# Moving the decay of v, the first state decays and most low weight halves of layer 1 from VectorE and ScalarE to GpSimd

## The chip, the cores and the metric

The kernel runs on one core of a Trainium2 chip. The metric is device time in microseconds (us) of one execution; a smaller number is better. Profiles are taken of one execution, and their times count from its first instruction. TensorE is called PE, VectorE DVE, ScalarE ACT, GpSimd POOL, and SyncE, which issues most transfers, SP.

## The reference, cut to what matters

```python
# q, k, v: (8, 8, 576, 64) f32;  w_in: (512, 2048), w_out: (2048, 512), both float64
scores = q @ k.T / 8
gamma = 1 - 2 ** (-5 - arange(8))                      # one per head
ret = scores * where(i >= j, gamma ** (i - j), 0)      # retention, no softmax
x = (ret @ v), heads side by side                      # 4608 tokens x 512
h = x @ moe_w_in;   x = (h - tanh(h)) @ moe_w_out      # layer 1
h = x @ moe2_w_in;  out = (h * sigmoid(1.702 h)) @ moe2_w_out   # layer 2
```

## The kernel before

**Retention.** A batch's 576 positions are cut into five chunks (four of 128, the last of 64), 40 chunks in all, worked off in order. For each chunk `att_load` issues transfers of kT, qT, v and k. `att_decay` multiplies v in place by one factor for each row and head (`dg`). `att_scores` multiplies q by k on PE into `pj` and masks the scores into `pm` on DVE (L321). `att_values` makes `op` on PE from the old state, `pm` and v (L334), makes the update `up` from k and v (L348), adds it to the state S (L352) and multiplies S by the decay over a chunk (L353); the next chunk's `op` reads that S. The result times `dq` becomes a part of x: kept in `xf` for the first 512 tokens (L362), else written through `xe` (L367) to `xd` in memory. The constant `LEAD` is 4: four chunks are done ahead of layer 1, the others piece by piece between its steps. In `att_decay` the first 8 chunks (2 * LEAD) are one DVE instruction each (L295); the later ones are 8 (in a batch's last chunk 4) ACT instructions (L300).

**Layer 1.** x is split into two f16 halves, `xh` (ACT, L186) and `xl` (DVE, L187); each weight likewise into a high half (`wih`, `woh`) and a low half (`wil`, `wol`), and each product takes three matmuls (L464 into h, L626 into y). Tokens go in nine tiles of 512; a tile has eight steps, and a step needs one pair of blocks of `w_in` (kind "i") and, two steps later, one of `w_out` (kind "o"). The weights arrive as 64-bit words of 1 MB for each of 16 units. `unit_load` issues the transfer into `f` (two buffers). `unit_join` puts the words together into f32 `w` (two buffers) with ACT (L176, for "o" also L180) and DVE (L178 for "i", L181, L182). `unit_split1` then makes the high half on ACT and the low half on DVE, through `two` (L186, L187). This conversion runs inside the first token tile: two units at each step until all 16 are done; two of the units come ahead of the first step. After tanh's on ACT (L477, L478), a step's `wt` is a DVE product (L482), and is split into `gh` (ACT) and `gl` (DVE).

**Order.** A planner puts each engine's instructions in a fixed order ahead of time, by the program's order and by when it expects operands to be ready. On the chip an engine works off its list in that order: an instruction whose operand is late holds up all behind it on its engine. `newest`, `pin` and `after` are tiny copies that make an instruction wait for another one's result, to hold it in its place. GpSimd has 18 instructions in the whole program; two of them (L158, tiny copies) hold back weight loads until a part of `xf` is there.

**Layer 2** starts near 830 us; its weights are converted by other functions, which the change leaves alone.

Of the kernel before, what the change touches and what calls it, by code (L numbers as in the profile page):

```python
# [17 lines left out]
AF = mybir.ActivationFunctionType  # L18
ALU = mybir.AluOpType
# [5 lines left out]
B, H, S, D = 8, 8, 576, 64  # L25
NT, DM, DFF = 4608, 512, 2048
P = 128
# [4 lines left out]
NPAIR = H // 2  # L32
CHUNKS = [(s0, min(P, S - s0)) for s0 in range(0, S, P)]
# [18 lines left out]
SW = 2.0**13  # L52
# [3 lines left out]
LEAD = 4  # L56
# [39 lines left out]
def small_h(ctx: ExitStack, tc: tile.TileContext, w1i, w1o, w2i, w2o, qt, kt, k, v, dq_d,  # L96
            dv_d, mask_d, dg_d, out, flag):
    nc = tc.nc
    V, A, G, PE, SP = nc.vector, nc.scalar, nc.gpsimd, nc.tensor, nc.sync
# [85 lines left out]
    def two(hi, lo, src, scale):  # L185
        A.activation(out=hi, in_=src, func=AF.Copy, scale=scale)  # L186
        V.scalar_tensor_tensor(out=lo, in0=src, scalar=scale, in1=hi, op0=ALU.mult, op1=ALU.subtract)  # L187

    def unit_split1(kind, p):
        o, w = L[1], L[1].raw.pop((kind, p))  # L190
        if kind == "i":
            b, u = divmod(p, 2)
            if not u:
                o.wih[b], o.wil[b] = (wp1.tile([P, KD, 512], F16, tag=f"{nm}{b}", name=f"{nm}1_{b}") for nm in ("wih", "wil"))
            hi, lo = (x[b][:, :, u * 256 : u * 256 + 256] for x in (o.wih, o.wil))
        else:
            b, u = divmod(p, 4)
            if not u:
                o.woh[b], o.wol[b] = (wp1.tile([P, 8, DM], F16, tag=f"{nm}{b}", name=f"{nm}1_{b}") for nm in ("woh", "wol"))
            hi, lo = (x[b][:, 2 * u : 2 * u + 2, :] for x in (o.woh, o.wol))  # L200
        two(hi, lo, w, SW)

    def unit_most1(kind, p):
        o = L[1]
# [61 lines left out]
    def ps_tile(pp, stage, name):  # L266
        p, tag = pp[stage]
        return p.tile([P, NPAIR, P], F32, tag=tag, name=name)

    def ps_two(pp, stage, name):  # L270
        p, tag = pp[stage]
        return p.tile([P, 2, NPAIR, P], F32, tag=tag, name=name)
# [17 lines left out]
    def att_decay(b, n):  # L290
        s0, T = CHUNKS[n]
        a = att[b, n]
        if b * len(CHUNKS) + n < 2 * LEAD:
            x, w = (0, H) if T == P else (H, NPAIR)
            V.tensor_tensor(out=a.v[:, :w], in0=a.v[:, :w], op=ALU.mult,  # L295
                            in1=dg[:, x : x + w].rearrange("p (a b) -> p a b", b=1).to_broadcast([P, w, D]))
            return
        for h in range(H if T == P else NPAIR):
            x = h if T == P else H + h
            A.activation(out=a.v[:, h], in_=a.v[:, h], func=AF.Copy, scale=dg[:, x : x + 1])  # L300

    def att_scores(b, n, pp, pin=None):
        s0, T = CHUNKS[n]
# [20 lines left out]
    def att_values(b, n, pp):  # L324
        s0, T = CHUNKS[n]
        a = att.pop((b, n))
        op = ps_two(pp, "v", "op")
        state = att.get((b, "S"))

        def add(w, x, c0, c1, start, stop):  # L330
            for hp in range(NPAIR):
                q, c = divmod(hp, 2)
                for j in range(2):
                    PE.matmul(op[64 * c : 64 * c + 64, j, q, c0:c1], w(hp, j), x(hp, j), start=start and not q, stop=stop and q == 1)  # L334

        half = lambda j: slice(64 * j, 64 * j + 64)
        if n:
            add(lambda hp, j: state[half(j), hp, :], lambda hp, j: a.qT[half(j), hp, :T], 0, T, True, False)
        if T == P:
            add(lambda hp, j: a.v[half(j), NPAIR * j + hp, :], lambda hp, j: a.p[j][half(j), hp, :64], 0, 64, not n, False)  # L340
            add(lambda hp, j: a.v[:, NPAIR * j + hp, :], lambda hp, j: a.p[j][:, hp, 64:], 64, P, False, True)
        else:
            add(lambda hp, j: a.v[half(j), hp, :], lambda hp, j: a.p[0][half(j), hp, :T], 0, T, not n, True)
        if n + 1 < len(CHUNKS):
            up = ps_tile(pp, "u", "up") if pp is not late else op[:, 0, 2:].rearrange("p a (b d) -> p (a b) d", b=2)
            for hp in range(NPAIR):
                for j in range(2):
                    PE.matmul(up[half(j), hp, :D], a.k[:, NPAIR * j + hp, :], a.v[:, NPAIR * j + hp, :], start=True, stop=True)  # L348
        if n + 1 < len(CHUNKS):
            new = ap.tile([P, NPAIR, D], F32, tag="S", name="S")  # L350
            if n:
                V.tensor_tensor(out=new, in0=up[:, :, :D], in1=state, op=ALU.add)  # L352
            V.tensor_tensor(out=new, in0=new if n else up[:, :, :D], op=ALU.mult,  # L353
                            in1=dg[:, H + NPAIR :].rearrange("p (a b) -> p a b", b=1).to_broadcast([P, NPAIR, D]))
            att[b, "S"] = new
        by_bank = lambda x, at: x.rearrange("p (j q) t -> p j q t", j=2)[:, :, :, at : at + T]
        done, g0 = 0, b * S + s0
        if g0 + T <= TT:

            if not x_first:  # L360
                x_first.append(yp.tile([P, KD, TT], F32, tag="yf", name="xf"))
            V.tensor_tensor(out=by_bank(x_first[0], g0), in0=op[:, :, :2, :T], in1=by_bank(dq, 0), op=ALU.mult)  # L362
            return
        e = ap.tile([P, NPAIR, P], F32, tag="xe", name="xe", bufs=1)
        if n + 1 < len(CHUNKS):
            V.tensor_copy(out=e[:, 0, :1], in_=new[:, 0, :1])
        V.tensor_tensor(out=by_bank(e, 0), in0=op[:, :, :2, :T], in1=by_bank(dq, 0), op=ALU.mult)  # L367
        while done < T:
            ti, off = divmod(g0 + done, TT)
            m = min(T - done, TT - off)  # L370
            SP.dma_start(x_d[ti][:, :, off : off + m], e[:, :, done : done + m])
            done += m
# [293 lines left out]
    dg = ac.tile([P, H + 2 * NPAIR], F32, name="dg")  # L666
# [11 lines left out]
    early = {"s": (ps_y, "y"), "v": (ps_a, "a"), "u": (ps_h, "h")}  # L678
# [3 lines left out]
    units1 = deque([("i", 0), ("i", 1), ("o", 0)])  # L682
# [8 lines left out]
    def next_join(after=None):  # L691
        unit_join(1, *units1[0], wb, after)
        next_load()

    def next_split():
        unit_split1(*units1.popleft())

    warm = cp.tile([P, TT], F16, name="warm")
    V.memset(warm, 0.0)
# [21 lines left out]
    for i in range(-2, LEAD):  # L721
        if i + 2 < LEAD:
            att_decay(*chunks[i + 2])
        if 0 <= i + 1 < LEAD:
            att_scores(*chunks[i + 1], early)
        if i >= 0:
            att_values(*chunks[i], early)
            if i == 0:
                att_load(*beyond[NIP])
                for x in range(2):  # L730
                    next_load(tp, x_first[0][:1, x, :1])
            if i in (1, LEAD - 1):
                fill(att[0, "S"][:1, 0, :1], 5 if i == 1 else 12)
        if i == 2:
            after = [att[0, LEAD - 1].p[-1][:1, 0, :1]]
# [2 lines left out]
        pre.popleft()()  # L738
    for i in range(2):
        next_join(after[i])  # L740
        next_split()
    for i in range(1, LEAD):
        att_load(*beyond[i + NIP])
    bg = deque()
    for i, ch in enumerate(chunks[LEAD:]):
        def begin(ch=ch, nxt=beyond[LEAD + i + NIP - 1] if i else None):
            if nxt:
                att_load(*nxt)
            att_decay(*ch)

        bg.append(begin)
        pp = middle if i < 2 else late
        pin = (lambda: att[0, "S"][:1, 0, :1], lambda: newest[0][:1])[i] if i < 2 else None
        bg.append(lambda ch=ch, pp=pp, pin=pin: att_scores(*ch, pp, pin))
        bg.append(lambda ch=ch, pp=pp: att_values(*ch, pp))
# [6 lines left out]
    for i in range(n1 + LAG):  # L762
        if i < n1:
            t, p = steps[i]
# [3 lines left out]
            for _ in range(2 if len(pre) > KF // 2 - p else 1):  # L768
                if pre:
                    pre.popleft()()  # L770
            work = [f for _ in range(2 if units1 else 0) for f in (next_join, next_split)]
            if bg:
                n = min(6 if t == 0 else 5, len(bg))
# [46 lines left out]
        if i >= LAG:  # L820
            t, p = steps[i - LAG]
# [4 lines left out]
    for n in range(LAG, NTILE * KF // 2):  # L826
        t, p = divmod(n, KF // 2)
# [827 lines left out]
```

## Time and profile before

| | us |
|---|---|
| median of 3 runs | 1558.76 (1558.08 to 1559.37) |
| the profiled execution: its own time | 1558.13 |
| its span, first to last instruction | 1556.4 |
| PE busy in the span | 1531.8 (98%) |
| DVE busy | 1082.1 (70%) |
| ACT busy | 823.1 (53%) |
| POOL busy | 4.9 (0%) |

The profiled execution's own time is 1.7 us over its span, and 0.6 us under the median of the runs. Busy shares are averages over stages with different limits; the time in which PE stands still is 24.6 us in the whole span.

### The profile page before, as it was taken

How to read it: one execution, taken by the hardware profiler on the slowest of the kernel's cores; microseconds unless marked ns; L12 is line 12 of the kernel's file. 1: busy time of each engine (PE TensorE's matmuls, PEld its weight loads, DVE VectorE, ACT ScalarE, POOL GpSimd, SP SyncE). 2: the span in 40 equal slices, each digit the busy share in tenths (PEclk: the TensorE clock that was granted, in tenths of full speed). 3: DMA queues.
4: the chain of work that ended last, by engine and by line, in shares of the span. 5: the costliest groups of instructions: out<-in, count | busy, mean ns of one | idle time of the engine just before them, and what ended most of it. 6: DMA issues, size and time to landing. Idle time of an engine off the chain costs nothing.

```text
span 1556.4 us, 29515 instructions
## 1 busy us (share of the span) xinstructions
PE 1531.8 (98%) x12347; PEld 1024.0 (66%) x12347; DVE 1082.1 (70%) x1720; ACT 823.1 (53%) x1441; POOL 4.9 (0%) x18
## 2 busy tenths in 40 slices
PE   7999999999999999999999999999999999999998
PEld 4444555555554544444444588888888888888887
DVE  6984535554443438888776499797888888887865
ACT  3995545455455446778676455354544454454432
POOL 0000000000000000000000000000000000000000
PEclk9999999999999999999999999999999999999999
DMA  9663324233323124444428243433434433432310
GB/s 356 219 197 123 118 74 155 73 105 109 112 79 106 51 92 138 170 162 156 158 101 310 85 150 116 152 123 123 150 119 127 141 127 119 140 129 99 133 62 30
DMA packets 107983, 205.84 MB, mean 132 GB/s; under 512 B 24640, under 2 KB 47808, under 8 KB 105664
## 3 DMA queue, kind: packets, MB, share of 16 engines
q1 hardware_dynamic: 107552, 203.72, 39.4%
q8 instruction: 99, 1.62, 0.4%
q14 instruction: 44, 0.36, 0.1%
q10 hardware_dynamic: 288, 0.14, 0.0%
HBM read 161.88 MB, written 41.94 MB: 131 GB/s over the span
## 4 chain that ended last, share of the span: by engine, by line
PE 91%; ACT 3%; DVE 1%; DMA 1%; issue 0%; ACTq 0%; SPq 0%; DVEq 0%
PE y L626 22%; PE h L464 22%; PE pr L520 21%; PE yp L555 20%; PE op L334 2%; PE pj L316 2%; PE yk L555 1%; PE op L348 1%; DMA f<-in_moe_w_out 1%; ACT w L176 1%; ACT v L300 0%; ACT u L481 0%; ACT u L477 0%; ACT wih L186 0%; ACT w L180 0%
## 5 line engine op out<-in xcount | busy, mean ns | idle before, releaser
L520 PEld LDWEIGHTS <-ws 128*128 128x128 f16 x3024 | 295.9, 98 | 36.5 <-issue 1.7
L464 PE MATMUL h<-xh,wih 128*128 128x512 f16 x576 | 218.2, 379 | 2.2 <-ACT wih L186 1.9
L464 PE MATMUL h<-xl,wih 128*128 128x512 f16 x576 | 218.2, 379 | 0.8 <-DVE xl L187 0.8
L626 PE MATMUL y<-gl,woh 128*128 128x512 f16 x576 | 218.5, 379 | 0.0
L626 PE MATMUL y<-gh,wol 128*128 128x512 f16 x576 | 218.4, 379 | 0.0
L464 PE MATMUL h<-xh,wil 128*128 128x512 f16 x576 | 217.9, 379 | 0.4 <-DVE wil L187 0.4
L626 PE MATMUL y<-gh,woh 128*128 128x512 f16 x576 | 218.2, 379 | 0.0
L520 PE MATMUL pr<-th,ws 128*128 128x256 f16 x1152 | 217.4, 273 | 0.3 <-DVE u L534 0.2
L626 PEld LDWEIGHTS <-woh 128*128 128x128 f16 x1152 | 112.2, 98 | 133.0
L464 PEld LDWEIGHTS <-wih 128*128 128x128 f16 x1152 | 111.0, 98 | 133.3 <-ACT wih L186 2.0
L482 DVE TENSOR_TENSOR wt<-u,wt 128x1024 f32<-128x1024 f32 x72 | 88.1, 1224 | 150.6 <-ACT u L481 150.6
L555 PE MATMUL yp<-wo,gh 128*128 128x256 f16 x1152 | 186.8, 273 | 0.0
L520 PE MATMUL pr<-bh,ws 128*128 128x256 f16 x864 | 170.4, 273 | 0.0
L477 ACT ACTIVATE u<-h 128x512 f32<-128x512 f32 x144 | 84.9, 590 | 158.2 <-PE h L464 158.1
L536 ACT ACTIVATE gs<-u,isig 128x1024 f32<-128x1024 f32 x72 | 82.5, 1146 | 142.6 <-DVE u L535 142.6
L520 PE MATMUL pr<-tl,ws 128*128 128x256 f16 x576 | 157.0, 273 | 0.0
L555 PE MATMUL yp<-wo,gl 128*128 128x256 f16 x576 | 135.4, 273 | 0.0
L186 ACT ACTIVATE gh<-gs,sg 128x1024 f16<-128x1024 f32 x72 | 82.7, 1149 | 91.5 <-DVE gs L539 91.3
L555 PE MATMUL yp<-wo,ringwoh 128*128 128x256 f16 x768 | 126.2, 273 | 0.0
L555 PEld LDWEIGHTS <-gh 128*128 128x128 f16 x1152 | 112.7, 98 | 13.0
L520 PE MATMUL pr<-bl,ws 128*128 128x256 f16 x432 | 117.4, 273 | 0.0
L186 ACT ACTIVATE gh<-wt 128x1024 f16<-128x1024 f32 x72 | 76.0, 1055 | 73.7 <-DVE wt L482 73.5
(141 smaller groups left out, 2317.7 us busy)
## 6 DMA issues: line engine op xcount, KB each, us to landing
ws<-pd SPq DMA_DIRECT2D x144, 448.0 KB, 3.9
f<-in_moe_w_in SPq DMA_DIRECT2D x16, 1024.0 KB, 5.8
f<-in_moe_w_out SPq DMA_DIRECT2D x16, 1024.0 KB, 5.1
yd<-ev SPq DMA_DIRECT2D x36, 256.0 KB, 2.6
yf<-yd SPq DMA_DIRECT2D x9, 1024.0 KB, 5.7
out<-ev SPq DMA_DIRECT2D x36, 256.0 KB, 2.6
kT<-t_k SPq DMA_DIRECT2D x32, 256.0 KB, 2.9
qT<-t_q SPq DMA_DIRECT2D x32, 256.0 KB, 2.8
```

What stands on the lines that cost most here:

```text
L176: A.activation(out=half[:, :, 1].bitcast(F16), in_=part[:, :, 3].bitcast(BF16), func=AF.Copy)
L186: A.activation(out=hi, in_=src, func=AF.Copy, scale=scale)
L316: PE.matmul(o, a.kT[hs, hp, :T], a.qT[hs, hp, :T], start=True, stop=True)
L334: PE.matmul(op[64 * c : 64 * c + 64, j, q, c0:c1], w(hp, j), x(hp, j), start=start and not q, stop=stop and q == 1)
L348: PE.matmul(up[half(j), hp, :D], a.k[:, NPAIR * j + hp, :], a.v[:, NPAIR * j + hp, :], start=True, stop=True)
L464: PE.matmul(h, w, x[:, kd, :], start=n == 0, stop=n == 3 * KD - 1)
L477: A.activation(out=u[:, x], in_=h, func=AF.Tanh, scale=isig * NARROW)
L482: V.tensor_tensor(out=w, in0=u, in1=th, op=ALU.mult)
L520: PE.matmul(ps, w, x[:, xi, k, :], start=i == 0, stop=i == 5)
L536: A.activation(out=gs.rearrange("p (a b) n -> p a b n", b=2)[:, 0:4:3], in_=h.rearrange("p (a b) n -> p a b n", b=2), func=AF.Gelu_apprx_s ...
L555: PE.matmul(bank[:, m], ops[a][:, x, m * P : m * P + P], L[2].out[w][:, p, wi, :], start=start and m == 0 and r == 0, stop=stop and m == 1 ...
L626: PE.matmul(ys[m], a, b, start=first and i == 0, stop=last and i == 2)
```

## The change

`att_decay` multiplies v on GpSimd for all chunks but the first one, in one instruction a chunk; the ACT form with eight pieces is gone. In `att_values` the product of S with the chunk's decay is GpSimd's for the second, third and fourth chunk. In `unit_split1` the pairs 0 and 1 of both kinds are split as before; for pairs 2 to 7 (12 of 16 units) the high half stays on ACT, and GpSimd first scales `w` in place and then subtracts the high half from it. Since the scaling overwrites `w`, it comes after ACT has read it. A one-element DVE copy makes the first unit's low half wait for the last column of `xf`.

```diff
-    def unit_split1(kind, p):
+    def unit_split1(kind, p, after=None):
...
-        two(hi, lo, w, SW)
+        if after is not None:
+            V.tensor_copy(out=lo[:1, 0, :1], in_=after)
+        if p < 2:
+            two(hi, lo, w, SW)
+            return
+        A.activation(out=hi, in_=w, func=AF.Copy, scale=SW)
+        G.tensor_scalar(out=w, in0=w, scalar1=SW, scalar2=None, op0=ALU.mult)
+        G.tensor_tensor(out=lo, in0=w, in1=hi, op=ALU.subtract)
...
-        if b * len(CHUNKS) + n < 2 * LEAD:
-            x, w = (0, H) if T == P else (H, NPAIR)
-            V.tensor_tensor(out=a.v[:, :w], in0=a.v[:, :w], op=ALU.mult,
-                            in1=dg[:, x : x + w].rearrange("p (a b) -> p a b", b=1).to_broadcast([P, w, D]))
-            return
-        for h in range(H if T == P else NPAIR):
-            x = h if T == P else H + h
-            A.activation(out=a.v[:, h], in_=a.v[:, h], func=AF.Copy, scale=dg[:, x : x + 1])
+        x, w = (0, H) if T == P else (H, NPAIR)
+        (G if b or n else V).tensor_tensor(out=a.v[:, :w], in0=a.v[:, :w], op=ALU.mult,
+                                           in1=dg[:, x : x + w].rearrange("p (a b) -> p a b", b=1).to_broadcast([P, w, D]))
...
-            V.tensor_tensor(out=new, in0=new if n else up[:, :, :D], op=ALU.mult,
-                            in1=dg[:, H + NPAIR :].rearrange("p (a b) -> p a b", b=1).to_broadcast([P, NPAIR, D]))
+            by = G if n and pp is early else V
+            by.tensor_tensor(out=new, in0=new if n else up[:, :, :D], op=ALU.mult,
+                             in1=dg[:, H + NPAIR :].rearrange("p (a b) -> p a b", b=1).to_broadcast([P, NPAIR, D]))
...
-    def next_split():
-        unit_split1(*units1.popleft())
+    def next_split(after=None):
+        unit_split1(*units1.popleft(), after)
...
-        next_split()
+        next_split(None if i else after[1])
```

## Rows read from the trace of the kernel before

**Rows 1.** Busy time of each engine by stretches of the span (us).

```profile
31.00:133.00 102.00, 94.90 (x745) 47.75 (x744) 87.11 (x109) 86.46 (x148) 0.00 (x0) 1.00 0.64 211
133.00:1540.00 1407.00, 1405.84 (x11180) 953.18 (x11179) 971.98 (x1572) 728.42 (x1283) 3.94 (x10) 1.00 0.37 122
```

**Rows 2.** Waits of PE from 0 to 135 us: total, times, longest.

```profile
PE op L334 <- DVE S L353: 4.1, 1, 4.1
PE op L334 <- DVE pm L321: 3.0, 2, 2.2
...
PE h L464 <- ACT wih L186: 1.9, 1, 1.9
```

**Rows 3.** Timeline, DVE, 21 to 25 us: start, duration, instruction.

```profile
21.01 0.41 DVE L352 TENSOR_TENSOR S<-up,S 128x256 f32<-128x256 f32 x1
...
23.73 0.43 DVE L295 TENSOR_TENSOR v<-v,dg 128x256 f32<-128x256 f32 x1 [2.25 <-DMA v<-n_v]
24.07 0.42 DVE L353 TENSOR_TENSOR S<-S,dg 128x256 f32<-128x256 f32 x1
```

**Rows 4.** Timeline, DVE, 36 to 38 us.

```profile
36.08 0.67 DVE L295 TENSOR_TENSOR v<-v,dg 128x512 f32<-128x512 f32 x1
36.67 1.21 DVE L182 SCALAR_TENSOR_TENSOR w<-f,w 128x1024 int32<-128x1024 int32 x1
```

**Rows 5.** Timelines of DVE and PE, 106 to 119 us.

```profile
106.84 1.21 DVE L187 SCALAR_TENSOR_TENSOR wil<-w,wih 128x1024 f16<-128x1024 f32 x1
...
115.88 1.22 DVE L187 SCALAR_TENSOR_TENSOR wol<-w,woh 128x1024 f16<-128x1024 f32 x1
...
108.75 1.16 PE L316 MATMUL pj<-qT,kT 64*128 64x128 f32 x16 [1.48 <-issue]
...
118.50 0.67 PE L334 MATMUL op<-qT,S 64*64 64x128 f32 x16 [2.22 <-DVE pm L321]
```

**Rows 6.** Timelines of DVE, PE and ACT, 49 to 76 us.

```profile
49.03 1.22 DVE L187 SCALAR_TENSOR_TENSOR wil<-w,wih 128x1024 f16<-128x1024 f32 x1
...
50.50 0.38 PE L464 MATMUL h<-xh,wil 128*128 128x512 f16 x1
...
73.25 1.22 DVE L187 SCALAR_TENSOR_TENSOR wil<-w,wih 128x1024 f16<-128x1024 f32 x1 [1.25 <-ACT wih L186]
...
75.63 1.39 ACT L176 ACTIVATE w<-f 128x1024 f16<-128x1024 bf16 x1
```

**Rows 7.** GpSimd's copies in the whole span, by shape: busy, mean ns.

```profile
L709 POOL COPY mask<-mask 64x64 f32<-64x64 f32 x2 | 0.5, 232 | 4.3 <-DMA mask<-c_mask 4.2
...
L158 POOL COPY f<-xf 1x1 int32<-1x1 int32 x2 | 0.3, 175 | 7.1 <-DVE xf L362 7.1
```

**Rows 8.** DVE's groups, 49.6 to 111.8 us: busy, mean ns.

```profile
L182 DVE SCALAR_TENSOR_TENSOR w<-f,w 128x1024 int32<-128x1024 int32 x10 | 12.2, 1224 | 0.7 <-ACT w L180 0.6
L181 DVE TENSOR_SCALAR f<-f 128x1024 int32<-128x1024 int32 x11 | 7.7, 701 | 1.8 <-ACT w L176 1.8
...
L482 DVE TENSOR_TENSOR wt<-u,wt 128x1024 f32<-128x1024 f32 x5 | 6.1, 1226 | 0.0
L187 DVE SCALAR_TENSOR_TENSOR gl<-wt,gh 128x1024 f16<-128x1024 f32 x5 | 6.1, 1220 | 0.4 <-ACT gh L186 0.4
...
L178 DVE TENSOR_SCALAR w<-f 128x1024 uint16<-128x1024 uint16 x5 | 3.8, 766 | 0.3 <-DMA f<-in_moe_w_in 0.3
```

**Rows 9.** ACT's pieces of v's decay, 49.6 to 111.8 us.

```profile
L300 ACT ACTIVATE v<-v,dg 128x64 f32<-128x64 f32 x24 | 6.2, 347 | 0.0
```

**Rows 10.** Timelines: GpSimd's reduction beside two kinds of DVE instruction.

```profile
940.95 0.68 DVE L539 TENSOR_TENSOR gs<-gs 128x512 f32<-128x512 f32 x1
...
941.12 0.72 POOL L137 PARTITION_ALL_REDUCE arx<-m  x1 [40.91 <-DVE m L395]
...
1084.61 0.41 DVE L535 TENSOR_TENSOR u<-pr,u 128x256 f32<-128x256 f32 x1
...
1084.86 0.35 POOL L137 PARTITION_ALL_REDUCE arx<-m  x1 [73.27 <-DVE m L395]
```

## The prediction

> **What bounds the kernel now.** I read busy time by stretches first. After 133 us PE stands still for 1.2 us in 1407 [rows 1], though ACT decays v and DVE works beside it: nothing that is taken off ACT or DVE there can shorten the run. From 31 to 133 us, the first token tile of layer 1, PE misses 7.1 us of 102 while DVE and ACT are both busy for some 85% and GpSimd does nothing [rows 1]. So what can be won lies ahead of 133 us, and the reader should look there for PE's waits, not for busy shares. The list of PE's waits has 4.1 us for a state, 3.0 us for masked scores and 1.9 us for a high weight half [rows 2]; the timeline adds 1.5 us before a score matmul at 108.75 [rows 5]. The sum of these four is 10.5 us, 0.7% of the run.
>
> The timelines then say what was late. At 21.42 the sum that makes the state was done, but its decay began at 24.07: the fifth chunk's v decay stood ahead of it in DVE's list and waited for its transfer until 23.73 [rows 3]. So the 4.1 us are mostly a queue, not work. The 1.9 us follow a weight join at 36.67 that had v decays ahead of it on DVE [rows 4]. The masked scores of 117 us stood behind a low half `wol` of 115.88, and the score matmul of 108.75 behind `xe`, which stood behind the `wil` of 106.84 [rows 5].
>
> **What each part of the change gives.**
>
> *The start.* The v decays leave DVE, so the state's sum is followed by what comes next. If GpSimd gets the state's decay before that v, the decay can begin 24.07 - 21.42 = 2.65 us earlier; if the planner puts v first on GpSimd too, the state gains nothing and only DVE's joins behind it move up. GpSimd's own price for a state's decay is not in the trace. Its lower end is DVE's 0.42 [rows 3]. For the upper end I take the copies: (232 - 175) / 63 = 0.90 ns for each element read, over 175 ns [rows 7]; with two operands read one after the other, 256 elements take 0.175 + 2 x 255 x 0.0009 = 0.63. Three of them cost between nothing and 0.6 us on the path. Between 0 and 2.65 I take 2.1, nearer the upper end because DVE's joins behind that v move up in either order, less 0.6 for the slower decays: 1.5 us won. The tiny copy that holds the first low half is 0.2 or less, by GpSimd's one-element copy [rows 7]; what stands behind it on DVE is that low half, and PE's first matmul with it; I take the 0.2. The two GpSimd copies that hold back weight loads may now stand behind a v decay that waits for its transfer, and SP's list behind them; bound 0 to 1 us, taken at 0.
>
> *The 1.9 us wait.* Two decays of 0.6 each (start to start 0.59 to 0.67 [rows 4]) leave DVE ahead of the join: 1.2 us won, from 0 to 1.9.
>
> *The later waits.* Taking the `wil` at 106.84 off DVE lets `xe`, and so the score matmul, come 1.1 us earlier of its 1.5 [rows 5]. Taking off `wol` at 115.88 lets the masked scores come 1.1 us earlier of 2.2 [rows 5]; the 0.8 us left of the 3.0 [rows 2] I count as 0.7 won. That is 2.9 us, from 0 to 4.5. What is late next is the planner's own order and the weights' transfers.
>
> *ACT.* Its decay pieces, 24 in 62 us for 6.2 us [rows 9], go. I count no time for that by itself: PE doesn't wait for them directly; it is a reserve for the conversion.
>
> *What GpSimd is given.* For a unit, a scaling and a subtraction of 1024 elements. The lower ends are DVE's 0.70 (L181) and 1.22 (L182) [rows 8], so 1.92. By the copies' slope the upper ends are 0.175 + 1023 x 0.0009 = 1.10 and 0.175 + 2 x 1023 x 0.0009 = 2.02, so 3.12. I take the upper end, for it comes from GpSimd itself. Against DVE's 1.22 a low half comes 0.7 to 1.9 us later after its high half. Who waits for it? For w_in, PE nearly at once: the `wil` made from 49.03 to 50.25 is read at 50.50 [rows 6]. But it waited on DVE then, and GpSimd is idle, so most of the difference is made good. For w_out there are two steps between. Then `w`: it has two buffers, and it is free when the low half is done, 73.25 + 1.22 = 74.47, while the join after next starts at 75.63 [rows 6]. That is 1.2 us of margin against 0.7 to 1.9, so 0 to 0.7 us for each of five pairs, 0 to 3.5 in all; behind the waiting join on ACT stand the tanh's that feed PE. DVE's and ACT's relief works against it. I take 1.0 us lost for this and `wil` together, near the low end, since the bound falls on conversions that run ahead of PE for most of the tile.
>
> The sum: 1.5 + 1.2 + 2.9 - 0.2 (the tiny copy) - 1.0 = 4.4 us won. Against the profiled execution's own time that is 1558.1 - 4.4 = 1553.7 (a span of 1552.0 and the same 1.7 around it); the median of the runs is 0.6 higher, so 1554.4 for a median.
>
> **A rule of the chip that speaks against it.** GpSimd and DVE may not be able to work at once. GpSimd's reduction took 0.35 beside a DVE sum with one operand from PSUM (`pr`), and 0.72 beside one with both operands in SBUF: it ended 0.21 us after that DVE instruction [rows 10]. That reads as a GpSimd instruction that had to wait for DVE; one case, and in it GpSimd is the loser, by 0.37 us. The Trainium skill, "SBUF — State Buffer", section "Who interferes with whom", says that a DVE instruction with two SBUF inputs, or in a two-port mode, and a GpSimd instruction that reads SBUF share a port as an exclusive lock: the second blocks until the first has ended. These rows agree for one direction; DVE blocked by GpSimd, no row here shows. By that rule all the work would add up as in the first rival below; by the one row alone only GpSimd's halves would slip.
>
> **The rivals.**
>
> *One at a time (slower).* From 49.6 to 111.8 us, which PE needs for five steps, DVE's instructions with all operands in SBUF that stay are 12.2 + 7.7 + 6.1 + 6.1 + 3.8 = 35.9 us [rows 8]. The 12 units come to 12 x 3.12 = 37.4, and three chunks' v decays (24 pieces [rows 9]) at 0.175 + 2 x 511 x 0.0009 = 1.09 each to 3.3. If none of these overlap, 76.6 us must fit into 62.2: 14.4 too many, less the 4.4 of waits that fill up, so 1558.8 + 10.0 = 1568.8. With the lower ends, 12 x 1.92 = 23.0 and 3 x 0.68 = 2.0, the sum is 60.9 and it just fits. It decides from the point where a unit costs (62.2 + 4.4 - 35.9 - 3.3) / 12 = 2.28 us. For it speak [rows 10] and the price that I took; against it, that only GpSimd was seen to wait, that w_out's low halves have two steps of slack, and that DVE's share in the sum contains single-operand instructions (L178, L181, 11.5 us) for which no row shows a conflict. The skill's "GPSIMD Engine Reference", section 3.1, gives 4497 ns for a two-input operation over 2048 f32 elements; as an estimate, half of it is 2.25 for the subtraction, and the sum above would grow by 2.8 us.
>
> *The queue only moves (no change).* The planner puts the waiting v ahead of the state's decay on GpSimd as it did on DVE; the start keeps its 4.1 us, and what is won later is given back through later low halves: 2.9 + 1.2 - 3.5 = 0.6 won, 1558.2. For it speaks that the same planner with the same transfers makes the order; against it, that DVE's joins no longer stand in that queue.
>
> *Everything is won.* The four waits of 10.5 us go: 1548.3. Against it: each has a next cause, and a transfer at the start can't come sooner.
>
> **How the numbers follow.** A change counts from 0.2%, 3.1 us, which is what a measurement of this kernel can tell from none. The forecast, with all that is won up to everything, spans 1548 to 1556 and gets 0.46. The moved queue, 1556 to 1562, gets 0.20. One at a time, 1562 to 1575, gets 0.34; I don't give it more, because its sum needs every instruction to exclude every other one. So: faster 0.46, same 0.20, slower 0.34. The likeliest is the forecast, and its sum of 1554.4 is the time I give; its own range is 1548 to 1556. Eight in ten must reach into the slower case up to its sum and its low end: 1549 to 1570, leaving about 5 in 100 below and 13 above.
>
> **What would show it.** Right: PE's first layer-1 matmul begins 1 to 3 us earlier; the wait for the state shrinks; DVE is busy for some 70 instead of 87 us between 31 and 133 (12 x 1.22 and three v decays fewer); GpSimd's scaling and subtraction take 1.1 and 2.0; the first tile ends 4 us earlier, and from there on all is shifted by the same amount. Wrong: GpSimd's subtractions of 3 us or more, or DVE's L182 and L187 that take 2 us or more in place of 1.2, while `wil` stands as what PE waits for; the second tile would then begin later than now. If the planner's expected times for GpSimd are off, PE's fixed order shows it as waits where there were none.

## The result, and the profile after

The changed kernel takes 1572.7 us (median of 4 runs, 1572.06 to 1573.24), the kernel before 1559.07 us beside it (4 runs). The ratio is 1.0087, 95% interval 1.0071 to 1.0103: slower by 13.6 us, where 4.4 us less was forecast. The time lies above the forecast's range (1548 to 1556) and above the wider one (1549 to 1570); nearest to it is the rival *One at a time* (1568.8, range 1562 to 1575).

**Where the time went.** Busy time by stretches, after (us: PE, weight loads, DVE, ACT, GpSimd, then granted clock, DMA share, GB/s); it answers to [rows 1]:

```profile
0.00:31.00 31.00, 21.07 (x321) 15.40 (x322) 12.27 (x22) 3.25 (x5) 7.35 (x15) 0.89 0.99 349
31.00:133.00 102.00, 93.53 (x720) 46.48 (x718) 85.81 (x92) 71.87 (x97) 61.34 (x27) 0.93 0.64 217
133.00:1540.00 1407.00, 1402.84 (x11100) 945.37 (x11099) 973.23 (x1569) 689.06 (x1105) 48.13 (x43) 1.00 0.37 122
```

From 31 to 133 us GpSimd is busy for 61.3 us, and ACT has 14.6 us less. DVE has only 1.3 us less (87.11 to 85.81), although twelve low halves of 1.22 us, 14.6 us, and v decays left it: what stayed on DVE has become longer. The granted clock of that stretch fell from 1.00 to 0.93. The span grew by 14.3 us (1556.4 to 1570.7): PE stands still for 30.2 us in place of 24.6, and is busy for 1540.5 in place of 1531.8 with the same 12347 matmuls. So 8.7 us of the 14.3 are not waits but longer matmuls. Busy time weighted by the granted clock, over stretches of 1 us up to 200 us, puts some 7 of them down to the lower clock (8.4 us lost to it after, 1.5 before); this is an estimate.

PE's waits, 0 to 160 us (total, times, longest):

```profile
PE up L350 <- POOL v L301: 5.9, 1, 5.9
PE h L467 <- ACT wt L481: 3.5, 2, 3.2
PE y L629 <- ACT gh L186: 2.7, 2, 1.8
PE h L467 <- DVE xl L187: 2.5, 1, 2.5
PE op L336 <- POOL S L356: 2.2, 1, 2.2
PE op L336 <- DVE pm L323: 1.3, 2, 0.7
```

Of [rows 2], the state's wait is shorter (4.1 to 2.2) and so is that for masked scores (3.0 to 1.3). Above them stand four that were absent before or under 1 us: for a v decay, a tanh's `wt`, a `gh` and an `xl`.

**The first new wait is at the start.** Timeline, GpSimd and then PE:

```profile
15.51 2.04 POOL L301 TENSOR_TENSOR v<-v,dg 128x512 f32<-128x512 f32 x2 [10.15 <-DMA v<-n_v]
...
23.73 0.61 POOL L301 TENSOR_TENSOR v<-v,dg 128x256 f32<-128x256 f32 x1 [3.85 <-DMA v<-n_v]
27.59 1.19 POOL L356 TENSOR_TENSOR S<-S,dg 128x256 f32<-128x256 f32 x1 [3.25 <-DVE w L171]
```

```profile
16.60 1.12 PE L350 MATMUL up<-v,k 128*64 128x64 f32 x16 [5.90 <-POOL v L301]
17.65 2.08 PE L318 MATMUL pj<-qT,kT 64*128 64x128 f32 x16
...
33.89 0.60 PE L467 MATMUL h<-xh,wih 128*128 128x512 f16 x2
```

GpSimd's first product begins at 15.51, though it names a transfer as what it waited for, and two decays that were ready then run back to back: that releaser had been done, and something else held GpSimd. How long can't be read from this trace, for part of the 10.15 us may be the transfer; in e1 below the same decay begins at 10.34, 5.2 us earlier. PE waits 5.9 us for it. The scores behind the wait take 2.08 us for the 16 matmuls that took 1.16 before, and the granted clock from 16 to 20 us is 0.50. The first matmul of layer 1 comes at 33.89; before it came at 30.83.

**The second is in the tile.** What ACT's joins wait for, 31 to 133 us, and one chain of it (ACT, then PE):

```profile
ACT w L176 <- POOL wol L208: 9.6, 4, 4.0
ACT w L176 <- POOL wil L208: 8.4, 5, 4.1
```

```profile
109.48 1.36 ACT L176 ACTIVATE w<-f 128x1024 f16<-128x1024 bf16 x1 [3.97 <-POOL wol L208]
110.71 1.33 ACT L180 ACTIVATE w<-f 128x1024 uint16<-128x1024 uint16 x1
111.91 1.03 ACT L206 ACTIVATE wih<-w 128x1024 f16<-128x1024 f32 x1
...
113.32 0.58 ACT L481 ACTIVATE wt<-h 128x512 f32<-128x512 f32 x1
```

```profile
113.96 0.59 PE L467 MATMUL h<-xh,wih 128*128 128x512 f16 x1 [3.22 <-ACT wt L481]
114.33 0.63 PE L467 MATMUL h<-xl,wih 128*128 128x512 f16 x1
114.76 0.63 PE L629 MATMUL y<-gh,woh 128*128 128x512 f16 x1
...
119.83 0.38 PE L629 MATMUL y<-gh,woh 128*128 128x512 f16 x1
120.05 0.38 PE L629 MATMUL y<-gl,woh 128*128 128x512 f16 x1
```

Nine joins wait 18.0 us in all for a `w` buffer that GpSimd still works in; before, none waited for a low half. Behind the join of 109.48 stand its second piece, a high half and the tanh's, and PE stands still for 3.22 us for the `wt` of 113.32. Then most matmuls start 0.43 us after the one before, and from 119.83 on 0.22 us: the engine runs at 1.2 GHz and then again at 2.4 GHz. The 14 steps from 113.96 to 119.83 take 5.87 us; at 0.216 each they would take 3.0. So this wait costs 3.2 us and 2.9 us more behind it. The windows show the same (columns as above):

```profile
112.00:116.00 4.00, 2.04 (x5) 0.81 (x6) 3.21 (x5) 4.00 (x9) 2.90 (x2) 0.62 0.99 346
116.00:120.00 4.00, 4.00 (x11) 1.47 (x10) 1.80 (x2) 2.10 (x4) 4.00 (x2) 0.53 1.03 376
```

**What GpSimd's work costs.** Its groups in the whole span (count, busy, mean ns, idle before):

```profile
L301 POOL TENSOR_TENSOR v<-v,dg 128x512 f32<-128x512 f32 x31 | 37.7, 1217 | 289.0 <-DMA v<-n_v 272.6 <-PE h L467 16.3
L207 POOL TENSOR_SCALAR w<-w 128x1024 f32<-128x1024 f32 x12 | 37.3, 3112 | 29.4 <-ACT wih L206 26.2 <-ACT woh L206 3.1
L208 POOL TENSOR_TENSOR wol<-w,woh 128x1024 f16<-128x1024 f32 x6 | 15.1, 2510 | 0.1
L208 POOL TENSOR_TENSOR wil<-w,wih 128x1024 f16<-128x1024 f32 x6 | 14.3, 2387 | 0.0
```

A unit costs 3.11 + 2.45 = 5.6 us in the mean, in place of 3.12. And the two engines hold each other up. Timeline, GpSimd and then DVE, the same stretch:

```profile
86.97 2.13 POOL L208 TENSOR_TENSOR wil<-w,wih 128x1024 f16<-128x1024 f32 x1
89.06 3.11 POOL L208 TENSOR_TENSOR wol<-w,woh 128x1024 f16<-128x1024 f32 x1
...
106.86 2.58 POOL L208 TENSOR_TENSOR wol<-w,woh 128x1024 f16<-128x1024 f32 x1
```

```profile
88.12 2.06 DVE L187 SCALAR_TENSOR_TENSOR gl<-wt,gh 128x1024 f16<-128x1024 f32 x1 [1.12 <-ACT gh L186]
90.11 1.27 DVE L323 TENSOR_TENSOR pm<-pj,mask 128x512 f32<-128x512 f32 x2
...
107.49 3.04 DVE L182 SCALAR_TENSOR_TENSOR w<-f,w 128x1024 int32<-128x1024 int32 x1
```

The `wil` ends at 89.10; the `gl` that was issued inside it ends 1.08 later, at 90.18, and the `wol` issued inside that ends at 92.17, 1.99 later. At the end of the stretch `wol` ends at 109.44 and the L182 behind it at 110.53, 1.09 later. Each looks as if it began only when the other engine's instruction had ended, and DVE's 1.22 us become 2.06 and 3.04. The masked scores of 90.11, which read PSUM, run beside `wol` in their usual time.

### The profile page after: what moved, and what is told of

The parts are those of the page before. It is cut to its first block, busy times and chain, and to the rows that moved or that the text cites. A ratio compares the mean times of both kernels' runs of the same rounds, so it can differ in the third digit from the quotient of the medians.

```text
span 1570.7 us, 29372 instructions
## 1 busy us (share of the span) xinstructions
PE 1540.5 (98%) x12347; PEld 1027.7 (65%) x12347; DVE 1084.3 (69%) x1699; ACT 771.2 (49%) x1213; POOL 116.8 (7%) x84
## 4 chain that ended last, share of the span: by engine, by line
PE 91%; POOL 2%; DVE 2%; ACT 1%; DMA 1%; issue 1%; SPq 0%; DVEq 0%; POOLq 0%
PE y L629 22%; PE h L467 22%; PE pr L523 21%; PE yp L558 20%; PE op L336 3%; PE pj L318 2%; DMA v<-n_v 1%; POOL w L207 1%; PE yk L558 1%; PE op L350 1%; DVE w L182 1%; DVE w L178 0%; POOL wil L208 0%; POOL v L301 0%; DVE f L181 0%
```

## The experiments

Each median is set against the kernel before on the same chip, whose medians lay between 1559.12 and 1559.50. Edits are shown against the kernel that the heading names. The letters are those of the expectations, each of which says in words what its theory holds. The time of the first layer-1 matmul comes from one execution a kernel; it is 32.11 in e11, whose total is that of before (30.83), so differences of some 1.3 us in it mean nothing by themselves.

**A product on GpSimd ahead of time (e1, against after).**

```diff
+    first = cp.tile([P, 2], F32, name="first")
+    G.memset(first, 0.0)
+    G.tensor_tensor(out=first[:, :1], in0=first[:, :1], in1=first[:, 1:], op=ALU.mult)
```

> The whole change, and ahead of it a two-element product on GpSimd at the very start of the program, so that GpSimd's first arithmetic no longer is the first v decay. Theory A (a one-time delay): in the changed kernel GpSimd stood still from 5.4 to 15.5 us although the first v had landed at 9.1, because its first arithmetic instruction has a one-time price; then the first v decay now begins near 10 us, the 5.9 us wait of PE is gone, layer 1 begins about 3 us earlier (33.9 to 31), and the time falls by 3 to 6 us, to 1567 to 1570. Theory B (the transfer or the order was late): the first decay stays near 15.5 and the time stays at 1572.7.

1568.08, ratio 1.0057 (1.0040 to 1.0073): 4.6 us of the 13.6 come back. The 5.9 us wait is gone, and the first layer-1 matmul comes at 32.25. 9.0 us of loss stay, so the start was about a third of it (the two ratios' intervals just touch, so the share is rough).

**One half of the change at a time (e2: splits on DVE; e3: all decays where they were; against after).**

```diff
 e2, unit_split1:
-        if p < 2:
-            two(hi, lo, w, SW)
-            return
+        two(hi, lo, w, SW)
+        return
 e3: att_decay and the state's product as before the change
```

> The decays of v and of the first states on GpSimd as in the change, all low halves on VectorE as before. Theory A (the start costs 3 to 6 us, the low halves the rest): 1560 to 1565, with PE's 5.9 us wait at the start still there and VectorE's joins at 1.2 us again. Theory B (the decays, spread over the whole first tile, are what holds VectorE up): 1568 or more. Rival C (the decays alone are a gain, since ScalarE is freed): below 1558.

> The low halves of pairs 2 to 7 on GpSimd as in the change, all decays on VectorE and ScalarE as before. Theory A (the low halves are most of the loss): 1566 to 1571, with VectorE's joins stretched to 1.4 us and more, and the lower TensorE clock between 31 and 133 us still there. Theory B (the start is most of it): 1558 to 1562.

e2: 1570.38, 1.0068 (1.0052 to 1.0085), first layer-1 matmul at 34.65. e3: 1568.86, 1.0063 (1.0046 to 1.0080), at 32.09. Either half alone loses 10 to 11 us, and both together 13.6: the parts don't add up. In e3 PE's new waits are for tanh's (`wt`, 3.2 us), `gh` (2.8) and `wil` (2.6); the granted clock from 31 to 133 us is 1.00, which the expectation had lower. e2 lies where its theory B put it, but e9 below gives 4.8 us of its loss back to the first product.

**The start put back (e4, against after).**

```diff
-        (G if b or n else V).tensor_tensor(
+        (G if b or n > LEAD else V).tensor_tensor(
...
-            by = G if n and pp is early else V
+            by = V
```

> The change, but the five v decays of the first batch and all state decays on VectorE, so that GpSimd has nothing on the path ahead of layer 1; its low halves and later decays stay. Theory A: layer 1 begins at 31 us or earlier, the time falls by 3 to 6 us, to 1567 to 1570, and what is left over the kernel before is the price of the low halves. If the low halves cost nothing, 1559 or less.

1568.07, 1.0054 (1.0037 to 1.0070), with the first layer-1 matmul at 30.88 as before. As much is left as in e1, 9.0 us, and it is lost inside the first tile: the first matmul of the second tile comes at 143.15, before at 132.71 (after: 147.96).

**Decays with the first product ahead (e9, against e2: e1's three lines added).**

> The decay-only run (decays of v and of the first states on GpSimd, low halves on VectorE) with the two-element product on GpSimd at the start. Theory A (decay-only loses its 11.3 us to the one-time price at the start and to TensorE's lower clock after the wait): PE's 6.4 us wait goes, layer 1 begins near 32 instead of 34.7, and 6 us or more come back: 1560 to 1564. Theory B (the decays lose it later, in VectorE's full first tile): 1567 or more.

1565.54, 1.0036 (1.0022 to 1.0050): 4.8 us better than e2, between what the two theories said. Its timeline of GpSimd at the start shows the price and where it lies, and the queue:

```profile
9.21 0.18 POOL L704 TENSOR_TENSOR first<-first 128x1 f32<-128x1 f32 x1 [8.38 <-issue]
...
23.85 0.61 POOL L300 TENSOR_TENSOR v<-v,dg 128x256 f32<-128x256 f32 x1 [7.70 <-DMA v<-n_v]
24.42 0.61 POOL L355 TENSOR_TENSOR S<-S,dg 128x256 f32<-128x256 f32 x1
```

A one-element product that waits for nothing begins 8.4 us after the instruction ahead of it. And the fifth chunk's v stands ahead of the state's decay on GpSimd as it did on DVE [rows 3]; PE waits 5.6 us for that state.

**Work on GpSimd that nobody waits for (e5: a scaling and a subtraction; e6: writes alone; against before).** Both add work to the kernel before and change nothing else: DVE's and ACT's instructions come in the same order as before as far as 115 us. One element of the high half lets the work begin.

```diff
+        if p > 1:
+            sa, sb = idly[0]
+            G.tensor_copy(out=sb[:1, :1], in_=hi[:1, 0, :1])
 e5:
+            G.tensor_scalar(out=sa, in0=sa, scalar1=0.5, scalar2=None, op0=ALU.mult)
+            G.tensor_tensor(out=sb, in0=sa, in1=sb, op=ALU.subtract)
 e6:
+            for x in (sb, sa, sa, sa, sa, sa):
+                G.memset(x, 0.0)
```

> The kernel before, and beside each of the 12 low halves that the change moves (which VectorE still makes) a scaling and a subtraction of 1024 elements on GpSimd, on two tiles that nobody else reads. They are gated by the unit's high half; no engine waits for GpSimd's results. Theory A (GpSimd's reads and VectorE's instructions exclude one another): VectorE's L178, L181, L182 and L187 are stretched as in the split-only run, by 12 to 20 us in sum over the first 150 us, and since VectorE here also keeps the 14.6 us of low halves, the time rises by 6 us or more, to 1565 or more. Theory B (what costs is that low halves come late from GpSimd): nobody waits for it here, so VectorE's durations and the time stay, 1557 to 1561.

> The same, but with six fills of 1024 elements with zeros on GpSimd for each unit in place of the scaling and the subtraction: GpSimd is busy for about as long and only writes. Theory A, as far as GpSimd's reads are what excludes two-operand instructions: VectorE's L182 and L187 stay near 1.22; L178 and L181 stretch only if writes exclude them as well; 1558 to 1562. Theory B: no change, 1557 to 1561. If any GpSimd instruction at all holds VectorE up, it comes out like the run with reads.

e5: 1576.44, 1.0111 (1.0094 to 1.0128); e6: 1564.73, 1.0045 (1.0028 to 1.0061). DVE's groups, 0 to 150 us, first of e5:

```profile
L182 DVE SCALAR_TENSOR_TENSOR w<-f,w 128x1024 int32<-128x1024 int32 x16 | 21.8, 1361 | 0.3
L181 DVE TENSOR_SCALAR f<-f 128x1024 int32<-128x1024 int32 x16 | 21.5, 1345 | 0.0
L187 DVE SCALAR_TENSOR_TENSOR wol<-w,woh 128x1024 f16<-128x1024 f32 x8 | 15.7, 1960 | 0.0
```

and of e6:

```profile
L182 DVE SCALAR_TENSOR_TENSOR w<-f,w 128x1024 int32<-128x1024 int32 x16 | 19.5, 1218 | 0.9 <-ACT w L180 0.7
L181 DVE TENSOR_SCALAR f<-f 128x1024 int32<-128x1024 int32 x16 | 16.4, 1023 | 1.6 <-ACT w L176 1.6
```

GpSimd's work, which nobody waits for, is enough to lose 17 us with DVE's and ACT's lists in their old order: contention by itself makes the kernel slower. Beside writes, the instructions with two operands keep their 1.22 us, and only those with one (L181, 0.70 before, and L178, 0.76 before and 1.14 here) grow. e6 is no clean measure of time, since many of its writes ran as early as 5 to 30 us. The Trainium skill, "SBUF — State Buffer", section "Who interferes with whom", says that a DVE instruction with two SBUF inputs contends with a GpSimd instruction that reads, and not with one that only writes, and that one in a two-port mode contends with both kinds. Both runs agree: L182 took 1361 ns beside reads and 1218 beside writes. L181 grew beside both kinds; that it runs in a two-port mode no run here shows.

**A cheaper unit and another buffer (against e4; e10: ACT scales, e13: three buffers for w, e15: w_in's low halves on DVE).**

```diff
 e10:
-        G.tensor_scalar(out=w, in0=w, scalar1=SW, scalar2=None, op0=ALU.mult)
+        A.activation(out=w, in_=w, func=AF.Copy, scale=SW)
 e13:
-    wb = pool("wb", 2, to=att_scope, side="right")
+    wb = pool("wb", 3, to=att_scope, side="right")
 e15:
-        if p < 2:
+        if p < 2 or kind == "i":
```

> The run with the start back on VectorE (1568.1), but w is scaled in place by ScalarE, and GpSimd only subtracts. GpSimd's work on low halves falls from 67 to some 30 us, ScalarE's rises by 12.6. Theory A (VectorE and GpSimd take turns, and the scaling is the larger part of it): VectorE's stretch at least halves, and the time falls by 4 us or more, to 1558 to 1564. Rival (late low halves through more steps in a row, whoever makes them): 1566 to 1572.

> The run with the start back on VectorE (1568.1), with three buffers for the joined weights w in place of two. Theory A (VectorE and GpSimd exclude each other, and the stretched VectorE is the loss): the stretch of L178, L181, L182 and L187 and the time stay, 1566 to 1570. Theory D (w is held until GpSimd has subtracted, so that the join after next waits): VectorE's 3.6 us of waiting for GpSimd's low halves goes, and 4 us or more come back, 1559 to 1564.

> The run with the start back on VectorE, but GpSimd makes only the low halves of w_out (six), which have two steps of slack; VectorE makes those of w_in. Theory A (turns at the port, by the amount of GpSimd's work): about half of the 9 us come back, 1562 to 1565. Theory E (the loss is that low halves of w_in reach PE late, by their own path): nearly all comes back, 1558 to 1561.

e10: 1572.33, 1.0075 (1.0058 to 1.0091). e13: 1573.90, 1.0100 (1.0083 to 1.0117). e15: 1568.01, 1.0059 (1.0042 to 1.0076). None is better than e4. In e10 a unit costs GpSimd only the subtraction, 2.14 us, and the loss is no smaller (the intervals of e10 and e4 overlap); but ACT, which makes the tanh's, is busy for 12.6 us more from 31 to 133 us. In e13 no join of ACT waits for a low half any more, but L182 takes 1563 ns in the mean and `wt` 2047, and PE's waits ahead of score matmuls come to 9.8 us: the 18 us of waits for `w` are how the loss reached PE, not why there was one. In e15 half of the units cost as much as all: DVE's `gl` takes 1802 ns and PE waits 8.0 us for `wt`. So neither the length of a unit, nor the buffers, nor w_in's low halves alone are the cause. Theory A, by which the loss goes with the amount of GpSimd's work, missed in e10 and in e15.

**Only the late decays, only the fifth, only the copy (against before).** e7 gives GpSimd the decays that ACT made, from the ninth chunk on; e8 the fifth chunk's v, with e1's lines; e12 both; e11 adds the one-element copy; e16 is e12 with three buffers for w.

```diff
 e8:
-            V.tensor_tensor(out=a.v[:, :w], in0=a.v[:, :w], op=ALU.mult,
+            (G if (b, n) == (0, LEAD) else V).tensor_tensor(out=a.v[:, :w], in0=a.v[:, :w], op=ALU.mult,
 e11:
+            V.tensor_copy(out=lo[:1, 0, :1], in_=after)
```

> The kernel before, with only the later v decays (from the ninth chunk on, which were eight pieces on ScalarE) as one GpSimd instruction each. The start and the low halves are as before. Theory A (start and low halves are the whole loss): within 1556 to 1560; ScalarE's 9 us in the first tile were a reserve only. Rival C (every GpSimd instruction beside VectorE costs): 1562 or more.

> The kernel before, with the fifth chunk's v decay alone on GpSimd and a two-element product on GpSimd at the start, so that the one-time price is paid early. In the kernel before that decay waited for its transfer at the head of VectorE's list, with the state's decay behind it, while PE stood still for 4.1 us. If that queue is the cause of the wait, layer 1 begins 1 to 2.6 us earlier and the time is 1555 to 1558; if the transfers set the start anyway, 1558 to 1560.

> The kernel before with the one-element copy alone that holds the first low half behind the last column of xf. All theories: 1557 to 1561, no change that can be measured; if it comes out 3 us or more slower, the single parts tried so far carried this copy's price too.

> The fifth chunk's v decay and all from the ninth chunk on on GpSimd, with the two-element product at the start; states, the other v decays and all low halves as in the kernel before. The fifth-only run began layer 1 3.4 us earlier and gave it back in the first tile. If ScalarE's load was what took it back, 1555 to 1558; if the weights' conversion on VectorE was, 1559 to 1562.

> The run with the fifth and the late v decays on GpSimd (1557.9), with three buffers for w. If the joins wait for w in the first tile of that run too, 1554 to 1557, and it beats both kernels; if they wait for the transfers into f, 1557 to 1560.

e7: 1559.83, 1.0005 (0.9996 to 1.0015). e8: 1560.56, 1.0010 (1.0000 to 1.0020). e11: 1559.21, 1.0000 (0.9991 to 1.0010). e12: 1557.85, 0.9993 (0.9984 to 1.0003). e16: 1561.43, 1.0013 (1.0003 to 1.0023). The copy and the late decays cost nothing that can be measured, and e16's third buffer wins nothing. e8 is the instructive one: with the fifth v alone out of DVE's queue, the first layer-1 matmul comes at 26.27, 4.6 us earlier than before (e12's expectation has 3.4, but the two timelines give 4.6), and nothing of it is left at the end; PE then waits 2.6 us for `xl`, 1.8 for `wil` and 1.7 for `wih`. e12 is the fastest of all kernels here, and can't be told from no change.

**Three decays in the first tile (e17: all from the sixth chunk on on GpSimd; e18: e7, and the products of chunks six to eight a second time on GpSimd; e19: e17 with those three left out).** e17 loses 6 us where e7 loses nothing, for three products more. Two causes were open, and each of two runs has only one of them: e18 the GpSimd work with e7's order of the other lists, e19 the order of DVE's and ACT's lists in e17 without the work.

```diff
 e17, against after: e4's edit, and e2's
 e18, against e7, behind DVE's product:
+            if b * len(CHUNKS) + n > LEAD:
+                G.tensor_tensor(out=idly[0][:, :w], in0=a.v[:, :w], op=ALU.mult,
+                                in1=dg[:, x : x + w].rearrange("p (a b) -> p a b", b=1).to_broadcast([P, w, D]))
 e19, against e17:
+        if LEAD < b * len(CHUNKS) + n < 2 * LEAD:
+            return
```

> All v decays from the sixth chunk on on GpSimd, the first five and the states' on VectorE, all low halves on VectorE. The late-decay run (from the ninth on) was 1559.8, the decay-only run with the early product 1565.5. If those 6 us are the three or four decays between 33 and 45 us, beside a VectorE that is full there, 1563 to 1566; if they are the first batch's decays and states, 1558 to 1561.

> The kernel with the decays from the ninth chunk on on GpSimd (1559.83, 1.0005 of before), and DVE keeps the decays of chunks six to eight; behind each of these three GpSimd makes the same product once more into a tile that nobody reads. The order of every other engine's list is as it was, so this holds the collisions of GpSimd with DVE at 33 to 43 us and nothing else. Theory F (contention: three GpSimd products beside DVE's joins stretch them by about 1 us each, and PE's waits and lower clock double that): 1563 to 1566, L181 or L182 between 33 and 45 us stretched by 0.5 to 1 us three times, waits of PE for wt. Theory G (order: with the decays gone from DVE's list the planner puts joins of the next weights ahead of a step's wt, which then comes 4 to 5 us later): 1559 to 1561, the same stretches but wt still near 42.4 us.

> The kernel with the decays from the sixth chunk on on GpSimd (1565.5, 1.0039 of before), with the decay of v of chunks six to eight left out altogether: DVE's and ACT's lists keep the order of that kernel, and GpSimd does nothing at 33 to 42 us. Left out are three products of 128x512. Theory F (contention): the loss goes, 1558 to 1561, first tile's wt and joins unstretched. Theory G (order): the loss stays, 1563 to 1566, with the first step's wt near 46 us in place of 42.4 although no DVE instruction before it is stretched.

e17: 1565.50, 1.0039 (1.0025 to 1.0053). e18: 1563.57, 1.0024 (1.0015 to 1.0033). e19: 1564.17, 1.0029 (1.0020 to 1.0038). Neither theory holds alone: contention by itself costs 4.1 us against before, the order by itself 4.7, both together 6.2. Timeline of e18, GpSimd and then DVE:

```profile
37.81 1.89 POOL L300 TENSOR_TENSOR sv<-v,dg 128x512 f32<-128x512 f32 x1 [0.69 <-DVE v L297]
44.41 1.89 POOL L300 TENSOR_TENSOR sv<-v,dg 128x512 f32<-128x512 f32 x1 [4.71 <-DVE v L297]
```

```profile
38.72 2.06 DVE L187 SCALAR_TENSOR_TENSOR wol<-w,woh 128x1024 f16<-128x1024 f32 x1
...
44.18 1.22 DVE L487 TENSOR_TENSOR wt<-u,wt 128x1024 f32<-128x1024 f32 x1
45.32 2.06 DVE L182 SCALAR_TENSOR_TENSOR w<-f,w 128x1024 int32<-128x1024 int32 x1
```

These two products stretch a DVE instruction by 0.84 us each, and a third, of 34.62, DVE's v decay of 36.47 by 0.5. PE then waits 2.45 us for `wih` and 1.28 for `wil`, and not for `wt` as expected; its clock from 40 to 50 us is 0.66 (in e7 1.00, with waits of 1.76 and 0.43). And e19's timeline of DVE:

```profile
43.33 0.70 DVE L181 TENSOR_SCALAR f<-f 128x1024 int32<-128x1024 int32 x1 [0.63 <-ACT w L176]
44.54 1.22 DVE L182 SCALAR_TENSOR_TENSOR w<-f,w 128x1024 int32<-128x1024 int32 x1 [0.51 <-ACT w L180]
45.69 2.06 DVE L486 TENSOR_TENSOR wt<-u,wt 128x1024 f32<-128x1024 f32 x1
```

Here nothing ahead of `wt` is stretched (it is itself, beside the ninth chunk's decay, which GpSimd begins at 45.59), yet it begins at 45.69; in e7 it begins at 42.40, 3.3 us earlier. 1.15 us of that go with the later first matmul of layer 1 in this execution (32.04 for 30.89). `wt` reads two squares `u` that ACT makes. ACT's timeline of e7, then of e19:

```profile
41.01 0.62 ACT L481 ACTIVATE u<-u 128x512 f32<-128x512 f32 x1
...
41.61 1.37 ACT L176 ACTIVATE w<-f 128x1024 f16<-128x1024 bf16 x1
```

```profile
43.15 1.36 ACT L180 ACTIVATE w<-f 128x1024 uint16<-128x1024 uint16 x1
44.36 0.62 ACT L485 ACTIVATE u<-u 128x512 f32<-128x512 f32 x1
```

In e7 the second square is done at 41.63, ahead of a join's pieces; in e19 it stands behind two of them and is done at 44.98. So with three decays gone from DVE's list, the order written ahead of time is another one on ACT too, and `wt` could not have begun before 45 us, whatever DVE did. How the late `wt` becomes the 4.7 us wasn't followed: e19's longest waits of PE come at 116.11 (3.92 us, ahead of a score matmul) and 89.86 (2.14, for a tanh).

## Why the prediction was wrong

**The step that failed** is the price of the low halves: "I take 1.0 us lost for this and `wil` together". e3, which has that part alone (with the tiny copy), lost 9.7. It failed in three places. The scaling was taken from the copies' slope at 1.10 and took 3.11 (no less than 2.77); the same slope was right for the two-operand products (v 1.09, took 1.04; subtraction 2.02, took 2.13 where DVE let it run). And the margin of 1.2 us for `w`, reckoned against a lateness of 0.7 to 1.9, met one of some 4 us and more (5.6 less DVE's 1.22), and it was counted for five joins, where nine wait, 18.0 us in all. And the stretching of DVE was in no term of the sum, only in a rival: e5, where nobody waits for GpSimd and DVE still makes the low halves, loses 17. "DVE's and ACT's relief works against it" was wrong for DVE: DVE was forecast at some 70 us for the stretch and is busy for 85.8.

**The rival that was right.** *One at a time* named the mechanism, and [rows 10] had shown it in one direction. It was given 0.34, against it that only GpSimd was seen to wait and that no row showed L178 and L181 in conflict. After shows DVE waiting too, and e5 and e6 show that one-operand instructions do conflict. Its sum was not right, and that it came within 4 us was luck: with a unit at its shortest rows, 2.77 + 2.13 = 4.9 us, it would be 35.9 + 12 x 4.9 + 3.3 = 98.0 us in 62.2, a loss of 31.4 after the 4.4. Neither does the sum with the subtractions alone fit, 35.9 + 12 x 2.13 + 3.3 = 64.8, no loss. What sets the time is not whether the work fits: e15 and e18 lose 9 and 4 us with much of the room left. The likelier reading, argued from their timelines and not tested by itself, is that it matters whether a stretched instruction stands ahead of a `wt`, `gl` or join that PE waits for next.

**The start, 1.5 us forecast as won.** The first layer-1 matmul came 3.1 us later, and e1 gives back 4.6 us of the time. The 8 us and more ahead of GpSimd's first product were in no term. With them paid ahead of time (e9) the queue moved as the second rival said. And the gain need not have lasted: e8's 4.6 us are gone by the end of the tile, where PE waits for `xl` and the first weights.

**The 1.9 us and the later waits, 4.1 us forecast.** The masked scores' 3.0 became 1.3, and neither the 1.9 us for `wih` nor the 1.5 us ahead of a score matmul is among PE's longer waits after. So those waits went, but other waits stand in their place, and no run has these steps alone: e10, e13 and e17 again wait 4 to 10 us ahead of score matmuls. The tiny copy, 0.2, can't be told from nothing in e11.

**What no term held: the clock behind a wait.** The sum counted a wait at its length. 8.7 of the 14.3 us are longer matmuls, some 7 of them by the lower clock, as behind 113.96. The trace of before has it too: behind the 4.1 us wait the 16 `op` matmuls take 1.13 us where they take 0.67 at 18.25, and the granted clock from 24 to 31 us is 0.76.

```profile
24.63 1.13 PE L334 MATMUL op<-qT,S 64*64 64x128 f32 x16 [4.13 <-DVE S L353]
```

**Open.** How much of the loss of after is contention and how much the changed order can't be divided: every edit that moves the splits changes both, and whether the two add even e17 to e19 can't tell (4.1 and 4.7 against 6.2, each good to 1.4 to 2.2 us). Why e13 is slower than e4 wasn't settled beyond its longer waits.

## What to carry to other kernels

Work given to an idle engine wasn't free here, even where nobody waited for it: look in the trace for pairs of instructions on two engines where one ends its own duration after the other, and take even one such pair as a reason to price every pair that the change would make. Take the duration of an operation only from rows of that operation on that engine, and have the engine's first call made before anything waits for it. Where lists are ordered ahead of time, a few short instructions taken off an engine's list can change what stands ahead of the one that the bound engine waits for, so look for the next wait before a won wait is booked.

## What the runs showed of the hardware that was not expected

- GpSimd's first arithmetic instruction begins late, once: 8.03 (e8) to 9.30 us (e5) after the instruction ahead of it where it waits for nothing, a one-element product or a scaling of 128x1024; its copies and memsets run before it without that. In after it is 10.15, part of which may be a transfer. Where the first product stands for long at the head of the list, the delay isn't seen: in e18 it begins at 34.62, 0.15 us after DVE has ended what it waits for, and GpSimd had been idle for 21.45. The Trainium skill, "GPSIMD Engine Reference", section 2.1, states some 6 us for the first call to freshly loaded code; the delay here is longer, and that it is this load no run shows.
- On GpSimd a scaling of 128x1024 f32 in place (2.77 us at least) takes longer than a subtraction of two such operands (2.13 us).
- After a wait of 3.22 us PE ran at 1.2 GHz for 5.9 us; after one of 5.90 us the granted clock was 0.50 from 16 to 20 us. In these two cases a wait of PE cost up to twice its length.
